# The first expert's last 1024 tokens as a unit with its output by seven products, its w2 sums formed during the second batch's attention

## The chip, the cores and the metric

One core of a Trainium2 chip runs the kernel. TensorE (PE) multiplies matrices, VectorE (DVE), ScalarE (ACT) and GpSimd (POOL) work element by element, and SyncE (SP) issues transfers, as POOL and ACT also do. The metric is the device time in microseconds (us) of one execution; the median of several runs is compared.

## The reference

Two stages. A block-sorted attention over 4 batches of 768 tokens, 8 heads of 64: per head an 8x8 matrix is balanced five times by rows and columns, it mixes the key and value blocks of 96 rows, and each query block attends to its mixed block. Its result, 3072 tokens of 512, goes to a mixture of 8 experts in which every token uses every expert:

```python
logits = x @ w_gate
P = np.exp(logits - logits.max())
for _ in range(8):
    P /= P.sum(1, keepdims=True) + 1e-09
    P /= P.sum(0, keepdims=True) + 1e-09
    P *= N / E
for e in range(E):
    h = np.maximum(x @ w1[e], 0.0)      # 512 -> 1024
    out += P[:, e:e + 1] * (h @ w2[e])  # 1024 -> 512
```

The gate weights P need the logits of all tokens, so they are known only some time after the last batch's attention.

## The kernel before

**Attention and the first expert.** Batches 0 to 3 go through attention one after another. While batches 1 to 3 are in it, PE fills up with the first expert's work for the batches that are ready: `hidden0` (four matmuls of 384 token columns per block of 128 features, and a ReLU by ACT) and `output0` (eight matmuls of 512 columns per tile of 128 tokens; the tile is copied to the accumulator `osbl` by `keep`, by DVE for the first 12 tiles, then by ACT). `first_two` does this for batches 0 and 1, woven into attention by `run_both` and `weave`.

**The stage that the change rewrites.** After attention, `last_two` does the first expert for batches 2 and 3. Beside it run three more generators, each advanced at given numbers n of one loop, `for n in range(56)`: `balance` (the eight rounds of row and column sums on the gate weights `glog`, called the Sinkhorn chain: five DVE operations, L600 to L604, one small f32 matmul with ones, L607, that sums over partitions, and three more on DVE, L608 to L611), the sums of token tiles (`sum_x`, L125 on DVE), and from n = 28 the first unit of expert 1, `units(1, 0)`. Tiles 18 to 23 are evicted already scaled by their weight (`keep_scaled`, L387); tiles 0 to 17 are scaled later by `scale0` (L745) on ACT.

**Experts 1 to 7** go in units of 1024 tokens, three per expert, by Winograd's scheme: 2x2 blocks, seven products in place of eight, in both layers. `hidden` issues a step per product (two matmuls of 512 columns); copies by ACT (L643, L651, L656, L665) and additions by DVE (L647, L659, L662, L669) put the blocks together. `output7` issues, for each of four i, seven products of four matmuls of 256 columns (L710); DVE multiplies by the gate weight and adds into `osbl` (`gather`, L675). Its operands are sums formed on POOL: of hidden tiles (`sum_h`, L693: three per i), of w1 (`sum_w`, L400) and of w2 (`sum_w2`, L573). In the main loop each product of the output is followed by one step of the next unit's hidden layer.

**What sets the order.** Nearly all PE instructions, and the sums and transfers of POOL, are pinned to program order (`pin`); the rest is ordered by the recording layer. Each engine executes its own queue in order, so an instruction that waits holds up all behind it. POOL's queue also issues transfers: the batches (`load_batch`), the weights, and half of the hops that carry the sorted values to other partitions (`hop`, L152). For batches 2 and 3 POOL also copies the query rows into the order that PE transposes (L180, inside `queries`).

**A gate.** At n = 40 POOL copies two columns of `glog` to `held` (L788); by its data that copy waits for the chain's last round, and the eight w2 sums of expert 1, issued next, stand behind it.

**Buffers.** w2 of expert 0 lies in pool `wcp`, those of experts 1 to 7 in two buffers of `wq`; w2 sums of odd experts in `w2q`, of even ones in the buffer of `wcp` that expert 0's w2 had.

Of the kernel before, what the change touches and what calls it, by code (L numbers as in the profile page):

```python
# [13 lines left out]
F32 = mybir.dt.float32  # L14
BF16 = mybir.dt.bfloat16
# [10 lines left out]
def kernel(  # L26
# [11 lines left out]
    nc = tc.nc  # L38
# [47 lines left out]
    def load_w2(e):  # L86
        w2t[e] = (wq if e else wcp).tile([128, 8, Dm], BF16, name="w2e")
        pin(nc.gpsimd.dma_start(out=w2t[e],
                                in_=moe_w2[e].rearrange("(fb k) f -> k fb f", k=128)))
# [76 lines left out]
    qT, kT, og = {}, {}, {}  # L166

    def queries(bb, hp, bank):

        qps = bank([128, 6, 128], BF16)  # L170
        if bb < 2:

            for kk in range(6):
                for h in range(2):
                    pin(nc.tensor.matmul(qps[64 * h:64 * h + 64, kk, :],
                                         qt[bb][:, 2 * hp + h, kk * 64:kk * 64 + 64],
                                         Ibig, is_transpose=True, start=True, stop=True))
        else:
            qr = sp.tile([128, 6, 2, 64], BF16, name="qr", bufs=2)
            nc.gpsimd.tensor_copy(  # L180
                qr.rearrange("p kk h d -> p h kk d"),
                qt[bb][:, 2 * hp:2 * hp + 2].rearrange("p h (kk d) -> p h kk d", d=64))
            for kk in range(6):
                pin(nc.tensor.matmul(qps[:, kk, :], qr[:, kk].rearrange("p h d -> p (h d)"),
                                     Ibig, is_transpose=True, start=True, stop=True))
        qT[bb, hp] = sp.tile([128, 128, 6], BF16, name="qTs", bufs=4)
        nc.scalar.copy(qT[bb, hp], qps.rearrange("p kk c -> p c kk"))
# [174 lines left out]

    def hidden0(c0, hTs, hbank, fbs=range(8)):
        for fb in fbs:
            hps = hbank()
            for kk in range(4):
                pin(nc.tensor.matmul(hps[:, 0:384], w1t[0][:, kk, fb * 128:(fb + 1) * 128],
                                     xtT[:, kk, c0:c0 + 384], start=(kk == 0), stop=(kk == 3)))
            nc.scalar.activation(out=hTs[:, fb, 0:384], in_=hps[:, 0:384], func=AF.Relu)  # L369
            yield  # L370

    def output0(c0, hTs, obank, done):
        for tt in range(3):
            oacc = obank()
            for fb in range(8):
                pin(nc.tensor.matmul(oacc, hTs[:, fb, tt * 128:(tt + 1) * 128],
                                     w2t[0][:, fb, :], start=(fb == 0), stop=(fb == 7)))
                if fb == 3:
                    yield
            done(c0 // 128 + tt, oacc)  # L380
            yield

    def keep(t, oacc):
        (nc.vector.tensor_copy if t < 12 else nc.scalar.copy)(acc(t), oacc)

    def keep_scaled(t, oacc):
        nc.scalar.activation(out=acc(t), in_=oacc, func=AF.Copy,  # L387
                             scale=glog[:, t, 0:1])

    wct = {}  # L390

    def sum_w(e):
        wct[e] = (wcq if e % 2 == 0 else wcp).tile([128, 3, 2, F // 2], BF16, name="wc")
        for kk in range(2):
            a11, a21 = (w1t[e][:, kk, f:f + 512] for f in (0, 512))
            a12, a22 = (w1t[e][:, 2 + kk, f:f + 512] for f in (0, 512))
            s1, s2, s4 = (wct[e][:, j, kk, :] for j in range(3))
            for a, b, o, c in ((a21, a22, ALU.add, s1), (s1, a11, ALU.subtract, s2),
                               (a11, a21, ALU.subtract, a21), (a12, s2, ALU.subtract, s4)):
                pin(nc.gpsimd.tensor_tensor(out=c, in0=a, in1=b, op=o))  # L400
                yield

# [79 lines left out]
    with ExitStack() as c2:  # L482
# [4 lines left out]
        def first_two():  # L487
            half = lambda: mps.tile([128, 8, 384], BF16, name="hTs")
            hA, hB = half(), half()
            for fbs in (range(4), range(4, 8)):  # L490
                yield from hidden0(0, hA, ebank, fbs)
                yield from hidden0(384, hB, ebank, fbs)
            yield from output0(0, hA, ebank, keep)
            yield from output0(384, hB, ebank, keep)
            for c0 in (S, S + 384):
                hTs = half()
                yield from hidden0(c0, hTs, ebank)
                yield from output0(c0, hTs, ebank, keep)

# [17 lines left out]
        load_batch(2, [(x, 0, 8) for x in "vkq"])  # L517
        build_r(2, nc.gpsimd, 4)
        run_both(at1, (1, 2, 1, 2))
        run_both(sort_values(2, bank1), (1, 0, 1, 0, 1))  # L520
        run_both(at1, (1, 0, 1, 0))
        usual = "q0,q1,k0 k1,s0,q2 k2,s1,q3 m0 k3,s2 m1,t0 s3 m2,t1 m3 t2 t3,l0 l3"
        for bb, ns in ((2, (5, 3, 2, 4)), (3, (5, 4, 0, 5))):
# [8 lines left out]
            weave(at1, ex, 3, ns[1])  # L532
            if bb + 1 < B:
                weave(sort_values(bb + 1, bank1), ex, 5, ns[2])
            else:
# [12 lines left out]
        tc.tile_pool(name=name, bufs=bufs, reuse_waits="tile"))  # L548
    mpc, xcp, wq, wcq = late("mpc", 1), late("xcp", 2), late("wq", 2), late("wcq", 1)
    osp = late("osp", 1)  # L550
    htp, fsp, hsp, w2q = late("htp", 2), late("fsp", 1), late("hsp", 3), late("w2q", 1)
    h3p = late("h3p", 2)
# [7 lines left out]
    def bank():  # L560
        return bk.tile([128, 512], F32, name="bk")

    w2s = {}

    def sum_w2(e):
        w2s[e] = (w2q.tile([128, 4, 4, Dm // 2], BF16, name="w2s") if e % 2 else
                  wcp.tile([128, 4, 4, Dm // 2], BF16, name="w2e"))
        for k in (0, 2):
            b11, b12 = (w2t[e][:, 4 + k:6 + k, d:d + 256] for d in (0, 256))
            b21, b22 = (w2t[e][:, k:k + 2, d:d + 256] for d in (0, 256))  # L570
            t1, t2, t3, t4 = (w2s[e][:, j, k:k + 2, :] for j in range(4))
            for a, b, c in ((b12, b11, t1), (b22, t1, t2), (b22, b12, t3), (b21, t2, t4)):
                pin(nc.gpsimd.tensor_tensor(out=c, in0=a, in1=b, op=ALU.subtract))  # L573
                yield

# [96 lines left out]

    def gather(e, t, c, ps):
        o = acc(t, c, ps.shape[-1])
        nc.vector.scalar_tensor_tensor(out=o, in0=ps, scalar=glog[:, t, e:e + 1], in1=o,  # L675
                                       op0=ALU.mult, op1=ALU.add)

# [16 lines left out]

    def output7(e, p, i, hT):
        a, b = 8 * p + i, 8 * p + 4 + i
# [11 lines left out]
        def add(ps, h, w, first):  # L708
            for fb in range(4):
                nc.tensor.matmul(ps, h[:, fb, :], w[:, fb, :], start=(first and fb == 0),  # L710
                                 stop=(fb == 3), skip_group_check=True)

        add(u, hT[:, 4:8, ha], b11, True)
        gather(e, a, 0, u)
        yield

        add(x0, hT[:, 0:4, ha], b21, True)
        yield
        add(u, s2, t2, False)
        gather(e, a, 256, u)  # L720
        yield
        add(x1, s1, t1, False)
        gather(e, b, 256, x1)
        yield
# [10 lines left out]
        add(u, hT[:, 0:4, hb], t4, False)  # L735
        gather(e, b, 0, u)
        if last and i == 3:
# [22 lines left out]

    def last_two():
        for bb, done in ((2, keep), (3, keep_scaled)):
            hT = htp.tile([128, 8, 1024], BF16, name="hT")
            halves = [(bb * S + c, hT[:, :, c:c + 384]) for c in (0, 384)]
            for c0, hTs in halves:
                yield from hidden0(c0, hTs, bank)
            for c0, hTs in halves:
                yield from output0(c0, hTs, lambda: op.tile([128, Dm], F32, name="oacc"), done)

    tail0, chain = last_two(), balance()  # L770
    x1, x2 = sum_x(1), sum_x(2)
    works = {0: x0, 10: x1, 14: x1, 19: x1, 23: x1, 41: x2, 43: x2, 46: x2, 48: x2}
    first = None
    for n in range(56):
        next(tail0)
        if n == 28:
            hT = htp.tile([128, 8, 1024], BF16, name="hT")
            first = units(1, 0, hT, pin)
        if first:
            next(first)  # L780
            if n == 28 + 21:
                sum_h(0, hT, 0, 3)
        if n in works:
            next(works[n], 0)
        if n in (0, 2, 4, 6, 8, 11, 13, 15, 17, 20, 22, 24, 26, 29, 31, 33, 35, 37, 39):
            next(chain)
        if n == 40:
            pin(nc.gpsimd.tensor_copy(held, glog[0:96, NT - 1, 0:2]))  # L788
            sums(8)
# [11 lines left out]
    for n in range(1, 3 * (E - 1) + 1):  # L801
# [6 lines left out]
        for i in range(4):  # L808
            if e == 1:
                scale0([t for t in (8 * p + i, 8 * p + 4 + i) if t < 18])  # L810
            if i == 0:
# [41 lines left out]
```

## Time and profile before

| | |
|---|---|
| median of 3 runs | 678.27 us (676.98 to 680.12) |
| profiled execution, its own time | 677.81 us |
| span from its first to its last instruction | 675.7 us |
| mean granted TensorE clock | 0.995 |
| attention with batches 0 and 1 of the first expert | 0 to 112.3 us of the span |
| rest of the first expert, Sinkhorn chain, first unit of expert 1 | 112.3 to 169.4 us |
| main loop of experts 1 to 7 | 169.4 us to the end |

A row of the timeline gives the start, the duration, the engine, the line of the kernel, the operation, what it writes and reads, and how many such instructions were merged; brackets hold the idle time of the engine ahead of it and whom it waited for. PE's durations overlap, since its matmuls are pipelined; the distance from start to start is what each one costs.

In windows of 50 us from 200 to 650 us PE is busy for 50.0 of 50; from 100 to 150 us for 48.98 and from 150 to 200 us for 49.33. POOL is busy for 9.87 us of 100 to 150 us and for 40.44 of 150 to 200 us.

### The profile page before, as it was taken

The page shows a single profiled execution, that of the slowest core. Times are in us where ns is not written, and L with a number is a line of the kernel's source. Part 1 is how long each engine was busy: PE and PEld are TensorE (multiplying, and loading weights), DVE is VectorE, ACT ScalarE, POOL GpSimd, SP SyncE. Part 2 cuts the span into 40 slices and gives each one's busy share as a digit, 9 for nine tenths or more (in the row PEclk, how much of TensorE's full clock was granted, in tenths as well). Part 3 has the DMA queues.
Part 4 walks back from the last instruction along what each step waited for, and adds up shares of the span by engine and source line. Part 5 has one row for each costly group of instructions (what it writes and reads, how often), then busy time and mean ns, then how long its engine had stood idle before and what let it go on. Part 6 is the DMA issues. An engine that isn't in the chain of part 4 may idle for free.

```text
span 675.7 us, 13246 instructions
## 1 busy us (share of the span) xinstructions
PE 658.8 (98%) x5127; PEld 435.1 (64%) x5127; DVE 542.3 (80%) x1133; ACT 297.4 (44%) x536; POOL 469.5 (69%) x494
## 2 busy tenths in 40 slices
PE   6899999999999999999999999999999999999996
PEld 3666666554666666666666666666666666666675
DVE  7527768673798888888898888888898888888896
ACT  4673863469434343333434343333434343333430
POOL 4702435007987998898997898689886999636745
PEclk9799999999999999999999999999999999999999
DMA  9996964002140340031303040034003120001223
GB/s 158 184 217 110 162 115 61 3 1 31 33 63 1 63 64 1 1 64 13 52 1 58 6 63 1 3 62 63 1 1 65 22 42 1 0 1 64 95 79 141
DMA packets 32735, 36.57 MB, mean 54 GB/s; under 512 B 2016, under 2 KB 25792, under 8 KB 32672
## 3 DMA queue, kind: packets, MB, share of 16 engines
q0 software_dynamic: 26672, 27.32, 25.7%
q1 hardware_dynamic: 5776, 8.20, 3.8%
q8 instruction: 40, 0.66, 0.4%
q10 hardware_dynamic: 224, 0.20, 0.1%
q14 instruction: 23, 0.19, 0.1%
HBM read 52.45 MB, written 6.29 MB: 87 GB/s over the span
## 4 chain that ended last, share of the span: by engine, by line
PE 72%; DVE 1%; POOL 1%; issue 0%; ACT 0%; DVEq 0%
PE oacc L710 36%; PE bk L623 35%; PE bk L710 1%; DVE osbl L675 1%; POOL hs L693 1%; DVE hT L659 0%; DVE hT L662 0%; ACT p L643 0%; DVEq L675 0%
## 5 line engine op out<-in xcount | busy, mean ns | idle before, releaser
L675 DVE SCALAR_TENSOR_TENSOR osbl<-oacc,glog,osbl 128x256 f32<-128x256 f32 (+1 forms) x490 | 255.5, 522 | 61.6 <-PE oacc L710 61.4
L623 PE MATMUL bk<-xtT,w1e 128*128 128x512 bf16 x504 | 149.8, 379 | 0.0
L693 POOL TENSOR_TENSOR hs<-hT 128x512 bf16<-128x512 bf16 (+2 forms) x105 | 99.3, 959 | 68.1 <-DVE hT L662 68.0
L710 PEld LDWEIGHTS <-hT 128*128 128x128 bf16 x1008 | 98.4, 98 | 64.6 <-issue 1.1
L710 PEld LDWEIGHTS <-hs 128*128 128x128 bf16 x1008 | 98.4, 98 | 64.7 <-POOL hs L693 1.5
L710 PE MATMUL oacc<-w2e,hT 128*128 128x256 bf16 x796 | 119.6, 273 | 0.5 <-ACT hT L665 0.5
L665 ACT ACTIVATE hT<-bk 128x512 bf16<-128x512 f32 x84 | 50.3, 598 | 158.6 <-PE bk L623 158.6
L693 POOL TENSOR_TENSOR hs<-hT,hs 128x512 bf16<-128x512 bf16 (+2 forms) x105 | 99.9, 959 | 4.9
L693 POOL TENSOR_TENSOR hs<-hs,hT 128x512 bf16<-128x512 bf16 (+2 forms) x105 | 99.9, 959 | 4.3 <-ACT hT L665 0.4
L623 PE MATMUL bk<-xc,wc 128*128 128x512 bf16 x336 | 100.0, 379 | 0.2 <-ACT p L643 0.2
L710 PE MATMUL oacc<-w2e,hs 128*128 128x256 bf16 x612 | 92.0, 273 | 0.9 <-POOL hs L693 0.9
L651 ACT COPY u<-bk 128x512 f32<-128x512 f32 x84 | 49.2, 586 | 95.2 <-PE bk L623 94.4
L623 PEld LDWEIGHTS <-w1e 128*128 128x128 bf16 x672 | 65.6, 98 | 10.5
L659 DVE CUSTOM_DVE_ANT_0 hT<-bk,p 128x512 bf16<-128x512 f32 x84 | 58.1, 692 | 11.5 <-ACT p L656 6.4
L669 DVE SCALAR_TENSOR_TENSOR h<-bk,hT 128x512 bf16<-128x512 f32 x84 | 57.2, 680 | 5.7 <-ACT hT L665 5.7
L656 ACT COPY p<-bk 128x512 f32<-128x512 f32 x84 | 49.2, 586 | 23.5 <-PE bk L623 23.5
L643 ACT COPY p<-bk 128x512 f32<-128x512 f32 x84 | 49.3, 587 | 20.1 <-PE bk L623 20.1
L647 DVE CUSTOM_DVE_ANT_0 hT<-bk,p 128x512 bf16<-128x512 f32 x84 | 57.2, 680 | 1.0 <-ACT hT L369 0.6
L662 DVE CUSTOM_DVE_ANT_0 hT<-bk,u 128x512 bf16<-128x512 f32 x84 | 57.1, 680 | 1.0 <-PE bk L623 1.0
L710 PE MATMUL oacc<-w2s,hs 128*128 128x256 bf16 x364 | 54.8, 273 | 0.1
L623 PEld LDWEIGHTS <-wc 128*128 128x128 bf16 x504 | 49.2, 98 | 8.0 <-issue 0.4
L623 PE MATMUL bk<-xtT,wc 128*128 128x512 bf16 x168 | 50.0, 379 | 0.0
(138 smaller groups left out, 831.5 us busy)
## 6 DMA issues: line engine op xcount, KB each, us to landing
w2e<-in_moe_w_dram POOLq DMA_DIRECT2D x8, 1024.0 KB, 8.9
w1e<-in_moe_w_dram POOLq DMA_DIRECT2D x7, 1024.0 KB, 8.3
out_dram<-osbl SPq DMA_DIRECT2D x23, 256.0 KB, 2.0
kvq<-in_v_dram POOLq DMA_DIRECT2D x3, 768.0 KB, 14.1
kvq<-in_k_dram POOLq DMA_DIRECT2D x3, 768.0 KB, 13.5
vsb<-vs SPq DMA_DIRECT2D x19, 97.5 KB, 5.4
kvq<-in_q_dram POOLq DMA_DIRECT2D x4, 384.0 KB, 10.8
kvq<-in_q_dram POOLq DMA_DIRECT2D x2, 768.0 KB, 21.8
```

The costliest lines, as they stand in the source:

```text
L623: hold(nc.tensor.matmul(ps, wa[:, kk, :], xa[:, kk, :], start=(first and kk == 0), stop=(kk == 1), skip_group_check=True))
L643: nc.scalar.copy(p1, u)
L647: nc.vector._custom_dve(TENSOR_ADD_SAT, out=c11, in0=w, in1=p1, s0=TOP, s1=0.0)
L651: nc.scalar.copy(u2, u)
L656: nc.scalar.copy(p5, v)
L659: nc.vector._custom_dve(TENSOR_ADD_SAT, out=c22, in0=u, in1=p5, s0=TOP, s1=0.0)
L662: nc.vector._custom_dve(TENSOR_ADD_SAT, out=c12, in0=v, in1=u2, s0=TOP, s1=0.0)
L665: nc.scalar.activation(out=c21, in_=u, func=AF.Relu)
L669: nc.vector.scalar_tensor_tensor(out=h3[e, p][:, i, :], in0=u, scalar=0.0, in1=c22, op0=ALU.max, op1=ALU.subtract)
L675: nc.vector.scalar_tensor_tensor(out=o, in0=ps, scalar=glog[:, t, e:e + 1], in1=o, op0=ALU.mult, op1=ALU.add)
L693: nc.gpsimd.tensor_tensor(out=c, in0=a, in1=b, op=o)
L710: nc.tensor.matmul(ps, h[:, fb, :], w[:, fb, :], start=(first and fb == 0), stop=(fb == 3), skip_group_check=True)
```

## The change

- The first expert's last two batches (1536 tokens) become 512 tokens in the old way (`before`: matmuls of 512 columns, four tiles) and a unit of 1024 (`hidden_last`, and `outputs`, which runs `output7` for expert 0). The hidden layer of that unit is plain, its output goes by seven products. DVE forms the fourth hidden operand (`h3`, one subtraction per block, L775), POOL the other sums (twelve more L701 operations of `sum_h`, in 15 instructions).
- `gather` for expert 0 copies the first contribution to each part of the accumulator on ACT (L681: 16 copies of 256 columns) and adds the second on DVE with weight 1.0. All 24 tiles are scaled later by `scale0`; `keep_scaled` is gone.
- The w2 sums of expert 0 (`sum_w2(0)`, eight POOL operations, L412) are issued during the second batch's attention, right after the loads of batch 2 and ahead of the query row copies. The first two row copies of each batch are pinned there (`rows`); on POOL they stand where they stood.
- The loop goes to 66. Expert 1's first unit starts at n = 24, the gate `held` and the w2 sums of expert 1 move to n = 12, and the chain's steps get new numbers. From n = 32 to 37 only the unit of expert 1 is issued; from n = 38 each step issues one output product of expert 0, and each even n a step of expert 1 besides.
- w2 of even experts lies in `wcp`, of odd ones in `wq`; the w2 sums have a buffer each beside them.

On PE the built program differs from before's only from this stage on; in the main loop only a few instructions per unit shift by a place or two. On POOL the order changes in one more place: in most units of the main loop, the last one among them, the first sum of the third i stood ahead of two of the short sums of the first i; now it stands behind them.

```diff
-        w2t[e] = (wq if e else wcp).tile([128, 8, Dm], BF16, name="w2e")
+        w2t[e] = (wq if e % 2 else wcp).tile([128, 8, Dm], BF16, name="w2e")
...
+    def rows(bb, hp):
+        qr[bb, hp] = sp.tile([128, 6, 2, 64], BF16, name="qr", bufs=2)
+        pin(nc.gpsimd.tensor_copy(
+            qr[bb, hp].rearrange("p kk h d -> p h kk d"),
+            qt[bb][:, 2 * hp:2 * hp + 2].rearrange("p h (kk d) -> p h kk d", d=64)))
...
-    def hidden0(c0, hTs, hbank, fbs=range(8)):
+    def hidden0(c0, hTs, hbank, fbs=range(8), n=384):
         for fb in fbs:
             hps = hbank()
             for kk in range(4):
-                pin(nc.tensor.matmul(hps[:, 0:384], w1t[0][:, kk, fb * 128:(fb + 1) * 128],
-                                     xtT[:, kk, c0:c0 + 384], start=(kk == 0), stop=(kk == 3)))
-            nc.scalar.activation(out=hTs[:, fb, 0:384], in_=hps[:, 0:384], func=AF.Relu)
+                pin(nc.tensor.matmul(hps[:, 0:n], w1t[0][:, kk, fb * 128:(fb + 1) * 128],
+                                     xtT[:, kk, c0:c0 + n], start=(kk == 0), stop=(kk == 3)))
+            nc.scalar.activation(out=hTs[:, fb, 0:n], in_=hps[:, 0:n], func=AF.Relu)
             yield
...
+    w2s = {}
+
+    def sum_w2(e):
+        w2s[e] = (wq if e % 2 else wcp).tile([128, 4, 4, Dm // 2], BF16, name="w2s")
...
+        for _ in sum_w2(0):
+            pass
+        for hp in range(2):
+            rows(2, hp)
...
-    def gather(e, t, c, ps):
+    def gather(e, t, c, ps, first=False):
         o = acc(t, c, ps.shape[-1])
-        nc.vector.scalar_tensor_tensor(out=o, in0=ps, scalar=glog[:, t, e:e + 1], in1=o,
-                                       op0=ALU.mult, op1=ALU.add)
+        if e == 0 and first:
+            nc.scalar.copy(o, ps)
+        else:
+            nc.vector.scalar_tensor_tensor(out=o, in0=ps, in1=o, op0=ALU.mult, op1=ALU.add,
+                                           scalar=glog[:, t, e:e + 1] if e else 1.0)
...
+    def hidden_last(hT):
+        h3[0, 2] = h3p.tile([128, 4, 512], BF16, name="h3")
+        for fb in range(8):
+            for c in (0, 512):
+                yield from hidden0(2048 + c, hT[:, :, c:c + 512], bank, (fb,), 512)
+            if fb > 3:
+                nc.vector.tensor_tensor(out=h3[0, 2][:, fb - 4, :], in0=hT[:, fb, 0:512],
+                                        in1=hT[:, fb, 512:1024], op=ALU.subtract)
+
+    def outputs(e, p, hT, hold):
+        for i in range(4):
+            if i < 3:
+                sum_h(i + 1, hT)
+            yield from output7(e, p, i, hT, hold)
+
+    def before():
+        hT = htp.tile([128, 8, 1024], BF16, name="hT")
+        yield from hidden0(1536, hT, bank, n=512)
+        yield from output0(1536, hT, lambda: op.tile([128, Dm], F32, name="oacc"), 4)
+
+    chain, x1, x2 = balance(), sum_x(1), sum_x(2)
+    works = {0: x0, 10: x1, 14: x1, 19: x1, 23: x1, 48: x2, 52: x2, 56: x2, 60: x2}
+    plain, one = before(), None
+    for n in range(66):
+        if n < 16:
+            next(plain)
+        elif n < 32:
+            if n == 16:
+                hT2 = htp.tile([128, 8, 1024], BF16, name="hT")
+                plain = hidden_last(hT2)
+            next(plain)
+            if n == 30:
+                sum_h(0, hT2, 0, 3)
+        elif n < 38:
+            if n == 32:
+                next(plain, 0)
+                sum_h(0, hT2, 3)
+                plain = outputs(0, 2, hT2, pin)
+        else:
+            next(plain)
+        if n == 24:
             hT = htp.tile([128, 8, 1024], BF16, name="hT")
-            halves = [(bb * S + c, hT[:, :, c:c + 384]) for c in (0, 384)]
-            for c0, hTs in halves:
-                yield from hidden0(c0, hTs, bank)
-            for c0, hTs in halves:
-                yield from output0(c0, hTs, lambda: op.tile([128, Dm], F32, name="oacc"), done)
-
-    tail0, chain = last_two(), balance()
-    x1, x2 = sum_x(1), sum_x(2)
-    works = {0: x0, 10: x1, 14: x1, 19: x1, 23: x1, 41: x2, 43: x2, 46: x2, 48: x2}
-    first = None
-    for n in range(56):
-        next(tail0)
-        if n == 28:
-            hT = htp.tile([128, 8, 1024], BF16, name="hT")
-            first = units(1, 0, hT, pin)
-        if first:
-            next(first)
-            if n == 28 + 21:
-                sum_h(0, hT, 0, 3)
+            one = units(1, 0, hT, pin)
+        if one and (n < 38 or n % 2 == 0):
+            next(one)
+        if n == 54:
+            sum_h(0, hT, 0, 3)
         if n in works:
             next(works[n], 0)
-        if n in (0, 2, 4, 6, 8, 11, 13, 15, 17, 20, 22, 24, 26, 29, 31, 33, 35, 37, 39):
+        if n in (0, 2, 4, 6, 8, 11, 13, 15, 17, 20, 22, 25, 27, 30, 32, 36, 38, 44, 46):
             next(chain)
-        if n == 40:
+        if n == 12:
             pin(nc.gpsimd.tensor_copy(held, glog[0:96, NT - 1, 0:2]))
             sums(8)
...
-                scale0([t for t in (8 * p + i, 8 * p + 4 + i) if t < 18])
+                scale0((8 * p + i, 8 * p + 4 + i))
```

## The prediction

> **What bounds the kernel now.** I read the busy shares and the chain that ended last first, then the timeline of PE through the stage that the change rewrites (112 to 172 us) and to the end, then VectorE (DVE) and GpSimd (POOL) beside it.
>
> ```profile
> PE 658.8 (98%) x5127; PEld 435.1 (64%) x5127; DVE 542.3 (80%) x1133; ACT 297.4 (44%) x536; POOL 469.5 (69%) x494
> PE 72%; DVE 1%; POOL 1%; issue 0%; ACT 0%; DVEq 0%
> ```
>
> PE is the bound, and the chain that ended last runs along it. A busy PE is no proof of a full one, so I take its pace from starts.
>
> ```profile
> 119.97 0.39 PE L607 MATMUL bk<-cs,onesc 128*128 128x8 f32 x2 [0.47 <-DVE cs L604]
> ...
> 153.89 1.03 PE L376 MATMUL oacc<-w2e,hT 128*128 128x512 bf16 x4
> 154.76 0.59 PE L623 MATMUL bk<-xc,wc 128*128 128x512 bf16 x2
> 155.19 1.03 PE L376 MATMUL oacc<-w2e,hT 128*128 128x512 bf16 x4
> ...
> 171.27 0.28 PE L710 MATMUL oacc<-w2e,hT 128*128 128x256 bf16 x1 [0.48 <-ACT hT L665]
> ...
> 172.17 0.60 PE L710 MATMUL oacc<-w2e,hT 128*128 128x256 bf16 x4
> 172.60 0.60 PE L623 MATMUL bk<-xc,wc 128*128 128x512 bf16 x2
> ...
> 660.74 0.28 PE L710 MATMUL oacc<-w2e,hs 128*128 128x256 bf16 x1 [0.89 <-POOL hs L693]
> ```
>
> Start to start, four matmuls of 512 columns take 0.866 us (0.2165 each), two 0.433, four of 256 columns 0.434 (0.1085 each); by the same reading 384 columns take 0.1625. From 172 us almost to the end the pattern runs without a gap, so a microsecond gained or lost on PE before 172 us arrives whole at the end. The stage from 112.33 to 169.43 us is 57.1: matmuls 128 x 0.1625 + 96 x 0.2165 + 56 x 0.2165 = 53.7, 1.9 of small f32 matmuls of the Sinkhorn chain, and waits. The waits, as gaps between starts: 0.10, 0.45, 0.65 and 0.44 (1.64) for the chain on DVE; 0.64 and 0.36 (1.0) at 171 us, behind ScalarE's (ACT's) queue; 0.22 and 1.05 (1.27) at 659 to 661 us, where PE waits for POOL's sums.
>
> **What the change removes.**
> (a) The output of eight token tiles: 64 x 0.2165 = 13.86 becomes 4 x 7 x 4 x 0.1085 = 12.15, -1.71. The hidden layers keep their columns (128 x 0.1625 = 20.80 against 96 x 0.2165 = 20.78): 0.
> (b) The Sinkhorn matmuls of the start stand 0.866 apart per step instead of 0.65. From one column sum to the next DVE needs 3.4 us (119.97 to 123.4); four steps gave 2.6, now 3.5. The waits go but for some 0.3 at the broadcast of the maximum, where one more 0.64 us x difference stands ahead on DVE: -1.3.
> (c) The 1.0 at 171 us: ACT's queue is refilled, see (g); I take it out here and count the new waits there.
> (d) At the end, the new POOL order puts the 1.11 us first sum of the third i behind the short sums of the first, where before's order has it ahead (656.15, three in one run). PE's 1.27 wait there shrinks by that: -1.1.
>
> **What it adds, without contention.**
> (e) Steps n = 32 to 37 hold products of expert 1's hidden layer alone. A product on a bank must wait for the copy of that bank: read latency 0.20 (PE to ACT elsewhere) + 0.58 copy - 0.43 for the one product between = 0.35. Four such places: 0.31 (the first behind a ReLU), 0.40, 0.06, and 0.43 for DVE's L659 kind: 1.2.
> (f) The seventh column sum stands at n = 38, 3.0 us of PE after the sixth (n = 32), 4.2 with (e). DVE has between them 2.6 of chain and three operations of 0.60 (hidden layer), and starts 0.9 late, behind the one of n = 32 and an h3 difference: 2.6 + 1.8 + 0.9 = 5.3: a wait of 1.2. Behind it on PE stands everything, since PE's order is fixed.
> (g) From n = 46 to the loop, 13 us, ACT's new order holds a dozen 256-column copies (0.30), six hidden evictions (0.49) and thirteen scalings (0.63 apart): 15 us. Copies stand behind scalings, and the next product on that bank waits for them: 0.87 between two products on a bank, 0.63 + 0.39 + 0.20 = 1.2 when a scaling is in front, so up to 0.35; place by place in the order 1.5 until the loop, 0.9 behind it (tiles 18 to 23 are scaled now too). 2.4 in all.
> Sum without contention: -1.71 - 1.3 - 1.0 - 1.1 + 1.2 + 1.2 + 2.4 = **-0.3 us**.
>
> Unseen durations: a 256-column ACT copy lies between 0.25 and the 0.586 of 512 columns; 384 columns take 0.49, so I take 0.39; the upper end adds 1.8, the lower takes 0.8 away. The 128x512 h3 difference on DVE: half of L125's 0.68 is taken, 0.68 adds 0.6.
>
> **Hidden parts.** The eight sums of the first expert's w2 (L573 kind, 9.2 us) go in front of the query rows on POOL. That w2 is issued at 26.55 and lands 20.9 later (the slower of its two landings): 47.4; done at 56.6. Behind them wait the two row copies, which waited for the q transfer until 59.10 anyway, four hop DMAs (64.08; POOL sat free for 3.4 before) and two more copies. So 2.5 + 3.4 us of lateness cost nothing; beyond that it shifts the hop one for one. DVE then reads PSUM only, and such rows keep their length beside POOL (L240 0.75 a pair at 65 and at 107 us). w2 of expert 2 now takes the buffer of expert 0, free at the stage's end and asked for 24 us later: 0. The twelve longer POOL sums of the new unit, 14 us, end well before the loop: at i = 1, 2, 3 they have 4.5 us each and need 3.45.
>
> **The term that decides: DVE beside POOL.** Before, the w2 sums of expert 1 waited for the Sinkhorn chain (L788, 39.7 us). Now they start after its third step, at about 123 us, and run beside it for 9 us; the new hidden sums run beside its last three rounds and the h3 differences. What a meeting costs, the trace shows twice:
>
> ```profile
> 61.41 0.68 DVE L125 TENSOR_TENSOR xc<-xtT 128x1024 bf16<-128x1024 bf16 x1
> ...
> 68.42 1.23 DVE L125 TENSOR_TENSOR xc<-xtT,xc 128x1024 bf16<-128x1024 bf16 x1
> ...
> 153.38 0.88 DVE L125 TENSOR_TENSOR xtT<-xtT 128x1024 bf16<-128x1024 bf16 x1
> ```
>
> ```profile
> 59.10 1.59 POOL L180 COPY qr<-kvq 128x768 bf16<-128x768 bf16 x2 [26.90 <-DMA kvq<-in_q_dram]
> ...
> 68.28 2.06 POOL L180 COPY qr<-kvq 128x768 bf16<-128x768 bf16 x2 [1.94 <-PE bank L184]
> ...
> 152.57 1.16 POOL L573 TENSOR_TENSOR w2s<-w2e,w2s 128x512 bf16<-128x512 bf16 x1
> 153.68 1.61 POOL L573 TENSOR_TENSOR w2s<-w2e 128x512 bf16<-128x512 bf16 x1
> ```
>
> L125 takes 0.68 alone and 1.23 or 0.88 where POOL was already running; 0.20 is just what POOL's sum of 152.57 had left at 153.38, and POOL's next one is longer by 0.45. So they take turns, whole operations at a time. The Sinkhorn multiplications (L603, L611) and h3 are of this kind, two inputs in SBUF; none ran beside POOL before. DVE operations with one input in PSUM kept their length through the loop. The Trainium skill, "SBUF — State Buffer", Who interferes with whom, says so too: two SBUF inputs on DVE and a reading GpSimd instruction exclude each other, and the later one blocks fully; both meetings agree.
> Ten such operations now meet POOL's 1.11 us sums, at half a sum each 5.5 us of DVE. Below: none of it counts (f32 chain operations are a quarter as long; they may slip through). Above: all of it. By place: the third column sum loses its 0.2 slack and 0.4; L659's kind at n = 35 stands behind two of them, +1.0; the seventh column sum +0.8; the first DVE add of the new output +0.4: **+2.6**, taken because the L125 rows are the same opcode.
>
> Sum: -0.3 + 2.6 = +2.3 on the profiled execution: 677.81 (span 675.7 + 2.1) becomes 680.1. The median shown is 0.46 above it, so 678.27 + 2.3 = **680.6 us**.
>
> **Rivals.**
> - No contention on the short f32 operations, so the saved columns stay: 678.27 - 0.3 = 678.0. For: no row shows them stretched. Against: same opcode, same kind of operands as L125.
> - Slower: the chain's 1e-9 additions (L601, one SBUF input, f32) are shut out by POOL as well. Four of them lie in the stretches where PE waits for the chain; each waits some 0.6 of a 1.11 sum, and as the chain is serial all but little reaches PE: +2.8, 683.4. It decides from a column sum that is already late, at n = 17, 38 and just behind. Against: rows with one SBUF input (L675) ran beside POOL unchanged, but those read PSUM as well. The same section of the Trainium skill counts tensor_scalar among those that take the shared ports in a two-port mode; no run here shows it.
> - The change doesn't do what it says: if (d) stays undone by a later POOL, +1.1 on any case.
>
> **Chances.** Forecast 0.42, the slower rival 0.30, no contention 0.22, anything else 0.06. Range 676.8 to 684.5: from the first rival with the fast copy to the second with a slow h3 and 0.5 of scatter. 0.5% (3.4 us) is about what a measurement of this kernel can tell from no change: faster 0.03; slower 0.31 (the slower rival and the upper edge of the forecast); same 0.66.
>
> **What would show it.** PE between the stage's start and the loop: 57 us grows to about 60, although its matmuls shrink by 1.7; waits at L612 (column sum) behind DVE at n = 17 and n = 38. L616 and L608 longer than 0.36 while POOL runs L412 or L701; L606 longer than 0.17 for the slower rival. PE waiting for ACT's L681 copies in the new output. The 0.89 at the end gone. From 180 us to 655 us nothing changes. Wrong if the stage shortens by over 1 us, if PE waits for hs in the new unit, or if the row copies of batch 2 start after 60 us.

## The result, and the profile after

The changed kernel takes 681.61 us (median of 22 runs, 678.70 to 682.94), the kernel before 678.31 (22 runs, 676.81 to 680.90): 1.0042 times as long, 95% interval 1.0029 to 1.0054, that is 3.3 us more. 2.3 were forecast.

Part of the difference between any two runs lies ahead of everything that was changed: TensorE's granted clock between 20 and 40 us differs from one profiled execution to the next. Below is the window of 20 to 30 us of the two profiled executions (busy time of PE, PEld, DVE, ACT and POOL with instructions in brackets, then PEclk, DMA share, GB/s), first before, then after:

```profile
20.00:30.00 10.00, 8.99 (x131) 6.83 (x128) 6.54 (x17) 8.41 (x13) 8.30 (x11) 0.84 0.90 164
```

```profile
20.00:30.00 10.00, 9.56 (x115) 7.74 (x111) 5.09 (x13) 7.59 (x12) 8.52 (x12) 0.55 0.95 168
```

From 30 to 40 us it is 0.83 before and 0.60 after. So the first matmul of the stage starts at 115.32 instead of 112.33 us in this execution (own time 682.89, span 681.1, clock 0.986), and 2.99 of its 5.1 us say nothing of the change: e2 below, which has all of the change ahead of the stage, starts it at 112.35 where that clock was 0.83 and 0.83. Runs of the changed kernel whose mean clock was 0.986 to 0.987 took 682.2 to 682.9 us, those at 0.996 to 0.997 took 678.7 to 679.9; the kernel before, in the later measurements, took 680.1 to 681.2 and 676.3 to 678.2 at these clocks. I therefore compare two distances inside each trace, read in the one profiled execution of each kernel, which this scatter does not touch: the **stage**, from the first hidden-layer matmul behind the attention to the first output product of expert 1, and the **path**, from that same matmul to the start of PE's last group of products. How well they repeat, two traces show: e1 and e5, whose program is that of before from the first output product of expert 1 on, lie a constant time behind it, within 0.01 us, from 175 us to the end.

| kernel | stage | path | median, ratio to before (95% interval) |
|---|---|---|---|
| before | 57.97 | 559.41 | 678.31 |
| after | 61.34 | 561.96 | 681.61, 1.0042 (1.0029 to 1.0054) |
| e1 before, early gate | 63.74 | 565.21 | 685.08, 1.0089 (1.0066 to 1.0113) |
| e2 after, late gate | 60.01 | 561.50 | 679.54, 1.0015 (0.9999 to 1.0030) |
| e3 after, plain output | 60.70 | 561.91 | 682.29, 1.0053 (1.0035 to 1.0072) |
| e4 before, order of POOL's sums | 57.95 | 559.40 | 679.52, 1.0006 (0.9990 to 1.0023) |
| e5 = e1, idle stretch filled | 60.75 | 562.20 | 681.12, 1.0036 (1.0015 to 1.0057) |
| e6 after, no row additions | 59.66 | 560.31 | 679.81, 1.0017 (0.9999 to 1.0035) |
| e7 = e2, chain spread wider | 57.94 | 561.03 | 680.96, 1.0037 (1.0019 to 1.0055) |
| e8 after, reordered | 56.93 | 558.37 | 676.45, 0.9979 (0.9961 to 0.9996) |
| e9 = e8, plain output | 56.83 | 557.89 | 676.44, 0.9978 (0.9959 to 0.9996) |

By the path the change costs 2.55 us: 3.37 in the stage, 0.82 won behind it.

From the page of the changed kernel, the busy shares and the chain that ended last:

```profile
PE 657.2 (96%) x5066; PEld 439.4 (65%) x5143; DVE 544.7 (80%) x1145; ACT 299.9 (44%) x542; POOL 493.6 (72%) x517
PE 70%; DVE 3%; ACT 2%; POOL 1%; issue 1%; POOLq 0%; DVEq 0%
```

PE is still the bound, with 1.6 us less of busy time, and a part of the chain has moved from it to its suppliers: DVE from 1% to 3%, ACT from 0% to 2%. Which waits those are, PE's timeline shows (start, duration, and in brackets the idle time and whom PE waited for):

```profile
133.20 0.39 PE L612 MATMUL bk<-cs,onesc 128*128 128x8 f32 x2 [1.08 <-DVE cs L609]
...
153.33 0.59 PE L628 MATMUL bk<-xc,w1e 128*128 128x512 bf16 x2 [0.79 <-DVE hT L664]
156.46 0.39 PE L612 MATMUL bk<-cs,onesc 128*128 128x8 f32 x2 [1.67 <-DVE cs L609]
160.44 0.60 PE L718 MATMUL oacc<-w2s,hT 128*128 128x256 bf16 x4 [0.53 <-DVE osbl L683]
```

All four wait for DVE: at the third and the seventh column sum, at a hidden-layer operation in the stretch that holds expert 1's products alone, and at an add of the new output. Why DVE is late at the third column sum, its timeline tells, with POOL's beside it:

```profile
129.20 1.08 DVE L616 TENSOR_TENSOR glog<-glog,cs 128x192 f32<-128x192 f32 x1
130.32 0.35 DVE L605 TENSOR_REDUCE rs<-glog 128x24 f32<-128x192 f32 x1
130.71 0.62 DVE L606 TENSOR_SCALAR rs<-rs 128x24 f32<-128x24 f32 x1
131.37 0.30 DVE L607 RECIPROCAL rs<-rs 128x24 f32<-128x24 f32 x1
131.70 0.92 DVE L608 TENSOR_TENSOR glog<-glog,rs 128x192 f32<-128x192 f32 x1
```

```profile
128.92 1.15 POOL L412 TENSOR_TENSOR w2s<-w2e 128x512 bf16<-128x512 bf16 x1
130.03 1.27 POOL L412 TENSOR_TENSOR w2s<-w2e,w2s 128x512 bf16<-128x512 bf16 x1
131.26 1.15 POOL L412 TENSOR_TENSOR w2s<-w2e 128x512 bf16<-128x512 bf16 x1
132.48 1.15 POOL L412 TENSOR_TENSOR w2s<-w2e,w2s 128x512 bf16<-128x512 bf16 x1
```

L616 and L608 take 0.36 where POOL is quiet, L606 0.18. Here the first ends at 130.28, L606 at 131.33 and L608 at 132.62, each 0.07 to 0.25 us behind the start of POOL's next sum, that is, just behind the end of the one that was running. The reduction (L605) and the reciprocal (L607) keep their 0.35 and 0.30; so does L613 (0.17), an addition too, but with its input in PSUM.

### The profile page after: what moved, and what is told of

Read it like the earlier page. It is cut to its first block, busy times and chain, and to the rows that moved or that the text cites. A ratio compares the mean times of both kernels' runs of the same rounds, so it can differ in the third digit from the quotient of the medians.

```text
span 681.1 us, 13243 instructions
## 1 busy us (share of the span) xinstructions
PE 657.2 (96%) x5066; PEld 439.4 (65%) x5143; DVE 544.7 (80%) x1145; ACT 299.9 (44%) x542; POOL 493.6 (72%) x517
## 4 chain that ended last, share of the span: by engine, by line
PE 70%; DVE 3%; ACT 2%; POOL 1%; issue 1%; POOLq 0%; DVEq 0%
PE oacc L718 36%; PE bk L628 33%; DVE osbl L683 1%; POOL hs L701 1%; DVE h L674 1%; ACT osbl L753 1%; ACT hT L670 1%; DVE hT L664 0%; ACT osbl L681 0%; DVE glog L608 0%; PE bk L718 0%; DVE hT L667 0%; POOLq L881 0%; ACT u L656 0%; DVE glog L616 0%
## 5 line engine op out<-in xcount | busy, mean ns | idle before, releaser
L683 DVE SCALAR_TENSOR_TENSOR osbl<-oacc,glog,osbl 128x256 f32<-128x256 f32 (+1 forms) x490 | 248.6, 522 | 61.8 <-PE oacc L718 61.8
L701 POOL TENSOR_TENSOR hs<-hT 128x512 bf16<-128x512 bf16 (+2 forms) x110 | 104.9, 962 | 80.5 <-DVE hT L667 66.5
L628 PE MATMUL bk<-xtT,w1e 128*128 128x512 bf16 x475 | 154.8, 379 | 1.4 <-ACT u L656 0.3
L718 PEld LDWEIGHTS <-hT 128*128 128x128 bf16 x1056 | 103.2, 98 | 66.1 <-issue 1.9
L701 POOL TENSOR_TENSOR hs<-hs,hT 128x512 bf16<-128x512 bf16 (+2 forms) x110 | 104.9, 962 | 5.7 <-ACT hT L670 0.8
L701 POOL TENSOR_TENSOR hs<-hT,hs 128x512 bf16<-128x512 bf16 (+2 forms) x110 | 105.0, 962 | 5.2
L718 PE MATMUL oacc<-w2e,hT 128*128 128x256 bf16 x684 | 102.4, 273 | 0.5
L718 PE MATMUL oacc<-w2s,hs 128*128 128x256 bf16 x684 | 102.1, 272 | 0.7 <-ACT osbl L681 0.2
L718 PE MATMUL oacc<-w2s,hT 128*128 128x256 bf16 x344 | 51.6, 273 | 0.6 <-DVE osbl L683 0.5
L718 PE MATMUL oacc<-w2s,h 128*128 128x256 bf16 x344 | 51.6, 273 | 0.5
```

The costliest lines, as they stand in the source:

```text
L628: hold(nc.tensor.matmul(ps, wa[:, kk, :], xa[:, kk, :], start=(first and kk == 0), stop=(kk == 1), skip_group_check=True))
L683: nc.vector.scalar_tensor_tensor(out=o, in0=ps, in1=o, op0=ALU.mult, op1=ALU.add, scalar=glog[:, t, e:e + 1] if e else 1.0)
L718: hold(nc.tensor.matmul(ps, h[:, fb, :], w[:, fb, :], start=(first and fb == 0), stop=(fb == 3), skip_group_check=True))
```

## The experiments

My theory (A): the loss is turn-taking of DVE and POOL in the Sinkhorn chain plus a crowded stretch from n = 32 on, and both come from where the work was put. The main rival (B): it is the new unit of seven products itself.

**e1: the kernel before with POOL's sums let go early.** PE, ACT and DVE have the work of before.

```
-        if n == 40:
+        if n == 12:
             pin(nc.gpsimd.tensor_copy(held, glog[0:96, NT - 1, 0:2]))
             sums(8)
```

> The kernel before with one thing of the change alone: expert 1's eight w2 sums on POOL are let go at n = 12 instead of n = 40; PE's, ACT's and DVE's work is as before. Theory A (turn-taking: POOL's 1.15 us sums shut out DVE's two-SBUF-input multiplications and its f32 additions of the Sinkhorn chain): L611 and L603, 0.36 alone, show 0.6 to 1.1 while the sums run, L601 0.5 to 0.65 instead of 0.18; the column sum of the third round, which does not wait in the kernel before, waits 2 to 4 us; stage start to first expert-1 output product 58.0 -> 60.0 to 62.0; time +2 to +4 us. Rival B (the loss of the change lies in its new unit of seven products and the crowded stretch from n = 32 on, the sums are absorbed by slack): L611 may stretch, but the third column sum waits under 0.5 and the stage stays 58.0 within 0.5; time within 0.5 us.

The stage grew by 5.77 us, more than even theory A gave. The third column sum waits as it said (in the kernel before it waits 0.28), but behind it PE is slow:

```profile
131.84 0.57 PE L607 MATMUL bk<-cs,onesc 128*128 128x8 f32 x2 [3.11 <-DVE cs L604]
132.26 7.22 PE L376 MATMUL oacc<-w2e,hT 128*128 128x512 bf16 x20
139.31 0.28 PE L607 MATMUL bk<-cs,onesc 128*128 128x8 f32 x2
```

From the third column sum to the fourth it takes 7.47 us; in the kernel before, 4.53 (127.06 to 131.59), with the same 20 matmuls between. So 2.83 of the 5.77 is DVE's lateness and 2.94 is slow matmuls. Rival B's "absorbed by slack" is out: with not one instruction of the new unit, the early sums alone cost more than the whole change. L601 took 1.12 once and 0.62 once (0.5 to 0.65 expected): once it waited for a whole sum.

**e5: e1 with the idle stretch filled.** Eight matmuls more, whose result nobody uses, ahead of the third column sum:

```
+            if it == 2:
+                idle = bank()
+                for _ in range(8):
+                    pin(nc.tensor.matmul(idle, w1t[0][:, 0, 0:128], xtT[:, 0, 0:512], ...))
             csps = bank()[:, 0:128]
```

> The kernel of e1 (before, with expert 1's w2 sums let go at n = 12) with eight matmuls of 512 columns more on PE, whose result is not used, right ahead of the third column sum, where PE stood idle for 3.11 us. In e1 the stage grew by 5.8 us although the third column sum is only 2.8 late; behind it the granted clock is 0.50 from 132 to 138 us. Theory A: that idle stretch took the clock down, and the clock took the other 2.9. The eight matmuls are 1.73 us long and lie wholly in the idle stretch: the wait falls to about 1.4, the granted clock stays 1.00 behind it, stage 63.7 -> 60.6 to 61.0, time -2.5 to -3.2 against e1. Rival: the clock fell for another reason (its place in the run); it is 0.50 again and the stage stays 63.7. Rival 2: the eight matmuls cost PE time of their own; stage 62.5 or more with the clock at 1.00.

PE's timeline and, below, the same window of both kernels (PEclk is the third number from the end), e5 first, then e1:

```profile
128.72 1.89 PE L609 MATMUL bk<-xtT,w1e 128*128 128x512 bf16 x8
131.92 0.39 PE L612 MATMUL bk<-cs,onesc 128*128 128x8 f32 x2 [1.30 <-DVE cs L604]
```

```profile
132.00:138.00 6.00, 6.00 (x31) 3.02 (x32) 4.47 (x12) 1.50 (x3) 2.68 (x3) 1.00 0.00 0
```

```profile
132.00:138.00 6.00, 6.00 (x16) 2.32 (x17) 3.12 (x8) 0.59 (x1) 2.51 (x3) 0.51 0.00 0
```

The column sum comes no later (17.49 us behind the stage's start against 17.55), the clock stays at 1.00 instead of 0.51, and stage and path fall by 2.99 and 3.01. More work made the kernel faster: in e1 the granted clock is half from 131.01 us, inside the idle stretch of 3.11, to 137.84, and that is paid besides the wait.

**e2: the changed kernel with POOL's sums let go late,** behind the chain.

```
-        if n == 12:
+        if n == 46:
             pin(nc.gpsimd.tensor_copy(held, glog[0:96, NT - 1, 0:2]))
```

> The changed kernel with expert 1's eight w2 sums let go at n = 46, behind the last chain step, instead of n = 12. Theory A: L616, L608 and L606 of rounds three to five are back at 0.36 and 0.18; the wait of 1.08 at the third column sum is gone; the seventh column sum still waits 1.0 to 1.7 (it is late behind the hidden layer's DVE work and POOL's new hidden sums); POOL's w2 sums end later by some 25 us, and the first hidden sums of expert 1 with them, so up to 0.6 comes back as a wait for POOL near the first expert-1 products. Stage 61.3 -> 59.8 to 60.6; time -0.5 to -1.5 us. Rival B: the third column sum's wait comes from the order of the steps and stays at about 1; stage and time within 0.4.

DVE in the third round, and where PE waits for POOL instead:

```profile
126.17 0.36 DVE L616 TENSOR_TENSOR glog<-glog,cs 128x192 f32<-128x192 f32 x1
...
126.94 0.18 DVE L606 TENSOR_SCALAR rs<-rs 128x24 f32<-128x24 f32 x1
```

```profile
175.85 0.50 PE L718 MATMUL oacc<-w2s,hs 128*128 128x256 bf16 x3 [1.02 <-POOL hs L701]
```

The stage lost 1.33 us, the wait at the third column sum is gone and the seventh stays at 1.67: theory A. But 1.02 (0.6 at most was expected) comes back as a wait for POOL, whose queue is now behind, and the path is only 0.46 shorter (0.5 to 1.5 expected).

**e6: the changed kernel without L606.** The line `nc.vector.tensor_scalar_add(rs2, rs2, 1e-9)` is taken out, and nothing takes its place.

> The changed kernel without L606, the additions of 1e-9 to the row sums: that part of the computation is left out. L606 takes 0.18 alone and 0.62 beside POOL's sums. Theory A (L606 is shut out by a running POOL sum as the multiplications are, the mechanism of the prediction's slower rival): L616 ends at 130.28, L606 at 131.33, L608 at 132.62 in the changed kernel, each just behind the end of a POOL sum; without L606, L608 can take the turn that L606 took, so the third column sum comes 0.8 to 1.1 earlier and its wait of 1.08 falls to 0.3 or less, the seventh's 1.67 to 0.7 to 1.2; stage 61.3 -> 59.5 to 60.4; time -0.9 to -1.8. Rival (only the multiplications are shut out, an addition costs its own 0.2 per round): third wait 0.7 to 0.9, seventh 1.3 to 1.5, stage 60.8 to 61.1.

The third column sum does not wait at all, and stage and path fall by 1.68 and 1.65, where an addition's own 0.2 (with the pause behind) would come to 0.4 in the two rounds that wait. So L606 does lose turns to POOL. At the seventh column sum I was wrong: 1.66 remains, since the multiplication behind it now meets a POOL sum for longer (L607 here; 1.28, against 0.92 in the changed kernel):

```profile
152.60 1.28 DVE L607 TENSOR_TENSOR glog<-glog,rs 128x192 f32<-128x192 f32 x1
```

One operation less saved no turn there, since the next one waited for the same POOL sum.

**e7: e2 with the chain's last steps further apart,** at n = 38, 42, 46, 50 instead of 36, 38, 44, 46.

> The kernel of e2 (changed kernel, w2 sums let go at n = 46) with the chain's last four steps at n = 38, 42, 46 and 50 instead of 36, 38, 44 and 46. Theory A (step (f): the seventh column sum stands on PE too soon behind the sixth; it is the spacing that makes it wait): the wait of 1.67 falls below 0.3, the rest stays (0.79 for L664, 0.3 to 0.6 for L683); POOL's w2 sums and the wait of 1.02 for its hidden sums near 176 us stay or grow by up to 0.5. Stage 60.0 -> 58.4 to 59.0, stage start to last product 561.5 -> 559.8 to 560.6, against 559.4 of the kernel before. Rival: the wait is only handed on to the next chain step or to L683, and the stage stays within 0.5 of 60.0.

No column sum waits any more, and the stage, 57.94, is as short as before the change. The path is not (561.03; 559.8 to 560.6 expected), as POOL takes most of it back. From PE's timeline:

```profile
168.87 1.03 PE L718 MATMUL oacc<-w2s,hs 128*128 128x256 bf16 x8 [0.34 <-POOL w2s L412]
...
176.69 0.28 PE L718 MATMUL oacc<-w2s,hs 128*128 128x256 bf16 x1 [1.66 <-POOL hs L701]
...
664.65 0.28 PE L718 MATMUL oacc<-w2e,hs 128*128 128x256 bf16 x1 [0.88 <-POOL hs L701]
```

The scheduler also chose the old order of POOL's sums at the end again (0.88).

**e3: the changed kernel with eight products for the last 1024 tokens,** and so without their sums and differences:

```
-                plain = outputs(0, 2, hT2, pin)
+                plain = output0(2048, hT2, lambda: op.tile([128, Dm], F32, name="oacc"), 8)
```

> The changed kernel with its last 1024 tokens brought to their output by eight products of 512 columns per tile (as the kernel before has it), in the same 28 steps; no h3 differences, no sums of the hidden layer on POOL; all else, the early gate too, as in the changed kernel. PE has 64 x 0.2165 instead of 112 x 0.1085: +1.7 of matmul. Theory A: the third column sum still waits about 1.1; the seventh waits 0.3 to 1.0 instead of 1.67, since POOL is quiet beside it; the waits for DVE's L683 (0.53) and the 0.16 for ACT go. Stage 61.3 -> 61.3 to 62.0; time 0 to +0.8: the seven products win back only what their own sums cost. Rival B (the new unit itself costs more than it saves): stage 61.3 -> 60.3 or less, time -1 or better. Rival C (the products' saving is whole): stage +1.7.

Stage 0.64 shorter although its matmuls are 1.71 longer; path 0.05 shorter. That lies between A and B: in this order the seven products save nothing and cost nothing. The seventh column sum still waits 1.38 (0.3 to 1.0 expected), with no operation on POOL beside it, so most of that wait is its place behind the sixth, not POOL.

**e4: the kernel before with POOL's hidden sums held to program order,** `pin(nc.gpsimd.tensor_tensor(...))` in `sum_h`.

> The kernel before with the POOL sums of the hidden layer held to the order in which the program issues them; nothing else. Step (d) of the prediction says that the wait of 1.27 us near the end (0.89 of it shown at the product of w2e and hs) comes from POOL's order, which the scheduler chose, and not from POOL's load: expected is that it shrinks to 0.4 or less and the time falls by 0.5 to 1.2 us, with the stage before 172 us unchanged. Rival: POOL is late at the end by its load whatever the order; the wait stays at about 1.2, time within 0.3.

```profile
662.63 0.61 PE L710 MATMUL bk<-w2s,hs 128*128 128x256 bf16 x4 [0.44 <-POOL hs L693]
```

The wait fell from 0.89 to 0.44, and the path not at all. The product of w2s and h at 229.48 us lies 1.71 later here, as the stage did; the one at 654.96 lies 2.54 later, and PE's last 1.71. What the end won, the loop had lost: 0.83, of which 0.26 is one wait at 521.6 us and the rest comes at about 0.01 with each output i. The place is PE's order in the loop, which the edit moved too, from 253 us on. A step of the next unit is two matmuls; here, once with each i, the first of the two stands one product (four matmuls) earlier, directly behind the step before it. The changed kernel has the same order. Its rows stand first, those of the kernel before below:

```profile
653.60 0.60 PE L628 MATMUL bk<-xc,wc 128*128 128x512 bf16 x2
654.04 0.38 PE L628 MATMUL bk<-xtT,w1e 128*128 128x512 bf16 x1
```

```profile
652.79 0.59 PE L623 MATMUL bk<-xc,wc 128*128 128x512 bf16 x2
653.22 0.60 PE L710 MATMUL oacc<-w2s,hs 128*128 128x256 bf16 x4
```

Such a matmul starts 0.228 us behind the last one, at 67 to 79 places of the loop; elsewhere a matmul of 512 columns takes 0.216. All six traces with that order (after, e2, e3, e4, e6, e8) drift so, and the five without it (before, e1, e5, e7, e9) do not; the same five have the wait of 0.88 or 0.89 at the end. So e4 does not show what POOL's order alone is worth: both orders changed together, and no run here parts them.

**e8: the changed kernel's work in another order.** Hidden layer of the 512 plain tokens, hidden layer of the 1024, then the plain output, which gives POOL time for its first sums, then one output product with one step of expert 1 at a time, as the main loop does:

```
...
+    for n in range(60):
+        if n == 8:
+            plain = hidden_last(hT2)
         if n == 24:
+            next(plain, 0)
+            plain = output0(1536, hT1, lambda: op.tile([128, Dm], F32, name="oacc"), 4)
+            sum_h(0, hT2)
+        if n == 32:
+            plain = outputs(0, 2, hT2, pin)
             hT = htp.tile([128, 8, 1024], BF16, name="hT")
             one = units(1, 0, hT, pin)
-        if one and (n < 38 or n % 2 == 0):
+        next(plain)
+        if one:
             next(one)
...
-        if n in (0, 2, 4, 6, 8, 11, 13, 15, 17, 20, 22, 25, 27, 30, 32, 36, 38, 44, 46):
+        if n in (0, 2, 4, 6, 9, 14, 15, 16, 19, 20, 24, 27, 29, 32, 33, 36, 39, 41, 45):
             next(chain)
-        if n == 12:
+        if n == 47:
             pin(nc.gpsimd.tensor_copy(held, glog[0:96, NT - 1, 0:2]))
```

> The changed kernel with the same work in another order: hidden layer of the 512 plain tokens (n = 0 to 7), hidden layer of the last 1024 (8 to 23), then the plain output of the 512 (24 to 31) while POOL forms the first sums, then the seven products together with expert 1's first unit, one step of each (32 to 59); chain steps spread over n = 0 to 45, expert 1's w2 sums let go at n = 47, behind the chain. No stretch is left in which expert 1's products stand alone. Theory A (the loss is contention, the product-only stretch and the place of the seventh column sum; the seven products save their 1.7): no wait over 0.8 but one of up to 1.6 at the fifth or sixth column sum; stage 56.0 to 58.0, start to last product 557.5 to 559.5 against 559.4 before and 562.0 after; time 676.5 to 679. Rival (the unit of seven products costs in ACT and DVE work what it saves on PE): start to last product stays 560.5 or more, time 680 or more.

In the numbers as theory A said: stage 56.93, path 558.37, 1.04 below before, and the median is below both kernels: 676.45 us, 0.9979 times before (0.9961 to 0.9996). So the loss was in the order, the late gate of the w2 sums included. Whether the seven products save their 1.7, as theory A also says, e8 alone can't tell. One column sum still waits, the sixth (the expectation of e9 calls it the fifth):

```profile
143.04 0.39 PE L612 MATMUL bk<-cs,onesc 128*128 128x8 f32 x2 [0.74 <-DVE cs L609]
```

**e9: e8 with eight products** for the 1024 tokens, in the same 28 steps.

> The kernel of e8 with the last 1024 tokens brought to their output by eight products of 512 columns per tile, spread over the same 28 steps; no h3 differences and no POOL sums for them. It asks what the seven products are worth in an order that leaves out the change's other costs. PE has 1.71 us more of matmul. Theory A (the saving is real, and in e8 partly paid by waits that the unit's own sums cause: 0.74 at the fifth column sum, beside POOL's sums): 0.74 goes, the rest stays; start to last product 558.4 -> 559.2 to 560.0, time +0.8 to +1.6 against e8. Rival (the unit of seven products gives back through DVE, ACT and POOL all it saves, even here): start to last product within 0.4 of 558.4, and the gain of e8 on the kernel before is that of its order alone.

The rival is right, by a little more than it said: with 1.71 us more of matmul the stage is 0.10 shorter and the path 0.48 (0.4 expected at most), and the median is the same (676.44). The round that waits in e8 does not here, and DVE's operations of that round keep their length; PE and DVE of e9, then DVE of e8:

```profile
142.03 0.28 PE L612 MATMUL bk<-cs,onesc 128*128 128x8 f32 x2
```

```profile
139.98 0.18 DVE L606 TENSOR_SCALAR rs<-rs 128x24 f32<-128x24 f32 x1
140.53 0.36 DVE L608 TENSOR_TENSOR glog<-glog,rs 128x192 f32<-128x192 f32 x1
```

```profile
140.54 0.62 DVE L606 TENSOR_SCALAR rs<-rs 128x24 f32<-128x24 f32 x1
141.54 0.92 DVE L608 TENSOR_TENSOR glog<-glog,rs 128x192 f32<-128x192 f32 x1
```

In both orders (e3, e9) the unit of seven products gives back all it saves. Of the 1.8 us that e8's stage waits longer, two waits make up 1.3 as gaps between starts (0.91 for the chain beside POOL's sums, 0.39 for ACT); the rest are gaps under 0.2 in the crowded 28 steps, which I did not take apart. The path understates the difference, since the two also differ in the loop: e8 has the order that loses there (0.9) and wins at the end (1.4), e9 neither. Up to the product of w2e and hs near 176 us e9 is 0.89 ahead. What makes e8 and e9 faster than before is thus not the seven products but what the two share: the order, with chunks of 512 tokens. Which part of it counts most was not tried.

## Why the prediction was right, point by point

The forecast, +2.3 us, is met by the path (+2.55). The measured time, 681.61, lies 1.0 above the 680.6 on record and within the range; by the comparison at equal clocks above some 2 belong to the change, and the rest of the medians' 3.3 goes with a lower clock. Of the 22 runs of the changed kernel 7 had a mean clock of 0.986 or 0.987, of 80 later runs of the kernel before 10; whether the change brings that about or chance, no run shows.

| term | forecast | measured |
|---|---|---|
| (a) fewer columns | -1.71 | -1.71 by count; no gain in time (e3, e9) |
| (b) Sinkhorn waits at the start | -1.3 | 1.64 to 0.18 = -1.46 |
| third column sum, contention | +0.4 | +1.24 |
| (e) with contention at n = 35 (+1.0) | +2.2 | 0.32 + 0.44 + 0.95 = +1.71 |
| (f) with contention (+0.8) | +2.0 | +1.84 |
| (g) to the loop, with the first DVE add (+0.4) | +1.9 | 0.70 at L683, 0.85 at five places behind ACT = +1.55 |
| (c) and (g) behind the stage | -0.1 | -0.33 |
| 187 to 655 us | 0 | +0.87 |
| (d) end | -1.1 | -1.36 |

Measured waits are gaps between starts beyond the pace of the matmuls, as in the prediction, so they are some 0.16 above the brackets. The trace after lacks 77 records of matmuls (5066 of PE against 5143 weight loads); where the loads show that one is missing, its 0.22 is not counted as a wait. The stage's terms add up to 3.17, the stage itself grew by 3.37; 0.2 is not accounted for.

That the sum comes out within 0.3 is in part luck. The third column sum and the loop cost 1.7 more than forecast, and six other terms, each 0.16 to 0.49 off, 1.65 less. And without L606 the path lies only 0.90 above before (e6), where the forecast, which let no addition wait, gave 2.3.

- **The deciding term stands.** DVE's multiplications beside POOL's sums were stretched from 0.36 to between 0.54 and 1.08, as the L125 rows had suggested; e1 and e2 show that POOL's sums do it.
- **Mis-sized: the third column sum,** 0.4 forecast, 1.24 measured. The prediction let only operations with two inputs in SBUF wait. The mechanism of its slower rival, additions shut out too, is there as well (L606 at 0.62, e6), so what happened lies between the forecast and that rival. The rival's price, 2.8, was too high: the two rounds that PE waits for gave 1.65 in e6, and the crowded rounds lose to POOL either way. On this the Trainium skill, "SBUF — State Buffer", Who interferes with whom, counts tensor_scalar among the operations that can take the shared ports; the trace agrees (0.18 alone, 0.62 beside POOL, and 0.17 unchanged where L613 reads PSUM), though it does not show the mode in which L606 ran.
- **(d)** came out, but "from 180 us to 655 us nothing changes" was wrong: the loop gave back 0.87, by PE's order there (under e4). So the wait at the end went, as said, but most of what that won did not arrive.
- **(a)** was counted as a gain of its own. In neither order tried it was one: the unit's sums, differences and copies on DVE, ACT and POOL took as much back (e3, e9).
- **Hidden parts** held: the first expert's w2 sums ran from 46.91 to 56.08 us (forecast 47.4 to 56.6), and the row copies behind them started at 58.60, waiting for the q transfer. The ACT copy of 256 columns takes 0.37 (0.39 taken), the h3 difference 0.41 alone and 0.53 to 0.60 beside POOL (0.34 taken).
- **The first rival** (no contention, 678.0) is out by e1 and e2.
- **Two slips of reading:** the parts of (f) add up to a wait of 1.1, not 1.2, and the POOL sum of 152.57 had 0.35 left at 153.38, not 0.20. Neither moves the forecast by more than 0.1.

## What to carry to other kernels

When work is moved to POOL, look at what DVE does beside it: here the short operations of a serial chain, those with two inputs in SBUF and the f32 addition in SBUF, waited until POOL's running operation was over (L606 0.62 and once, in e1, 1.12 us in place of 0.18), so the chain's price went by POOL's durations, not by DVE's. A saving in matmul columns is not yet a gain: the engines that make the operands and take the results can give it all back; test it by putting the plain form into the same order (e9). And look at the length of each idle stretch of PE: one of 3.11 us cost 2.94 more than itself, those of up to 1.67 in this stage did not; where between them the limit lies, no run here shows.

## What the runs showed of the hardware that was not expected

An idle stretch of 3.11 us took PE's granted clock to half for 6.83 us (0.51 from 132 to 138 us), which cost 2.94 us beyond the wait itself (e1), and about half as much idle (1.30 in e5; 1.67 in the changed kernel) left it at 1.00. The Trainium skill, "TensorE: Matmul & The Clock Gate", The HAM clock gate, says that the clock is halved after an idle window of about 3.4 us, and that the windows run freely. The traces agree on the window: but for the one at the very end, the stretches of half clock last 3.41, 6.83, 10.24 or 17.07 us, multiples of 3.41. But here 3.11 us of idle, a little less than a window, was enough. And the clock between 20 and 40 us goes with the start of the stage: over the eleven profiled executions it starts between 111.01 us (e8, clock 1.00 there) and 115.50 (e3, 17.07 us of half clock), a difference larger than the change.

A second thing is the hidden matmul that stands directly behind the step before it in the loop: it starts 0.228 us behind the last one, against 0.216 (under e4). Why, no run here shows.
